# Windowed attention with sinks, then a gated MLP: another layout for keys and queries, turned in quarters, and another order of the stages

## The chip, the cores and the metric

The kernel runs on one core of a Trainium2 chip. The metric is the device time of one execution in microseconds, as a median of several executions. The core has TensorE (PE, matrix products; its weight loads are listed as PEld), VectorE (DVE), ScalarE (ACT), GpSimd (POOL) and SyncE (SP, which here issues DMAs). Each engine works through its own instructions in order and waits for others through semaphores.

## The reference

There are 4 batches with 8 heads, 768 positions and head dimension 64, all in float32. Each query sees the first 4 positions (the sinks) and its own 128 latest positions. The heads are put side by side to rows of 512 and go through a gated MLP with 1536 hidden columns.

```python
scores = scale * np.matmul(q, k.transpose(0, 1, 3, 2))
pos = np.arange(S)
is_sink = pos[None, :] < int(n_sink)              # n_sink = 4
rel = pos[:, None] - pos[None, :]
in_window = (rel >= 0) & (rel < int(window))      # window = 128
scores = np.where(is_sink | in_window, scores, -1000000000.0)
scores = scores - np.max(scores, axis=-1, keepdims=True)
a = np.exp(scores)
a = a / (np.sum(a, axis=-1, keepdims=True) + 1e-09)
attn = np.matmul(a, v)
x = attn.transpose(0, 2, 1, 3).reshape(B * S, H * D)
out = (np.maximum(x @ w_gate, 0.0) * (x @ w_val)) @ w_out
```

## The kernel before

**Units and stages.** A unit is a pair of heads of one batch; there are 16, four per batch, and unit i has batch i // 4. "Stage i.x" below is stage x of unit i. Every unit passes through these stages.

*Load and cast.* `load_kq` (L88) and `load_v` (L93) issue DMAs on SP: keys and queries as 96 partitions with 8 rows of each head (two runs of 2 KB per partition), V as seven overlapping tiles of 128 rows, 256 bytes a row, in three DMAs. `cast_kq` (L108) and `cast_v` (L102) turn them into bfloat16 on POOL. `cast_v` also copies the four sink rows of V into tiles 1, 3 and 5 (L106), on ScalarE for units 0 to 3 and on POOL later. There are three buffers for `kf` and `qf`, two for `kn` and `qn`, four for the others.

*T, the turn (L167).* TensorE turns keys and queries, so that the 64 dimensions of both heads lie on 128 partitions: 8 transposes for the keys and 8 for the queries, each of 96 partitions by 128 columns (L172). ScalarE copies the keys out of PSUM into `kE` (L178 to L181), where each block of 124 keys has the four sink columns ahead of it (L182 copies those). VectorE copies the queries into `qT` (L177).

*S, the scores (L185), in three groups g.* TensorE multiplies `kE` and `qT` per head, with 64 partitions of the array each and the two heads in two PSUM banks (L195). ScalarE takes the exponential (L199), VectorE multiplies with a mask (L201). For units 0 to 3 no such product is made; a bias is put into PSUM by a matmul first (L191).

*V, the output, in two halves of 384 columns (L205).* TensorE multiplies the weights `ee` with V and with ones (L212), one head in each column half of the array, first all products with V and then all with ones. VectorE turns the sums, takes the reciprocal, turns it back and multiplies (L218 to L222) into `xT`, the rows for the MLP. V 0 needs S 0 and S 1, and V 1 needs S 1 and S 2.

**PSUM.** Two pairs of banks, `PP`, serve T, S and V in turn; each stage takes the next pair by `pair()` or `two()`. S and V take one, while T takes two, one for the keys and one for the queries, and uses half of each. So a stage waits until the stage that used its pair has been read out. In the head T and V take single banks from `G` instead. `G` serves the MLP afterwards.

**MLP.** `chunk(b, g, m)` (L227) makes 128 hidden columns for 384 rows of batch b: four matmuls for the gate (L234), Relu on ScalarE (L237), four for the value (L239) and the product into `hT` on VectorE (L241). Its fourth matmul needs `xT` of the fourth unit. `ffn2` (L248) is one matmul of the last layer (L254); after twelve of them ScalarE copies the result (L258) and SP stores it (L259).

**Order.** The program order is written out by hand. First comes the head: T, S 0, S 1 and V 0 of units 0 to 3, S 2 of units 0 and 1, and the weight loads between them. Then 96 slots follow. Each slot holds one chunk, then the stages that `plan` gives it, then up to three `ffn2` matmuls (there are none before slot 24). Slots 0 to 5 hold what is left of units 0 to 3, V 3.1 in slot 5. The list `later` holds the stages of units 4 to 15, and its first 24 entries are spread over slots 6 to 23, the others go one to a slot:

```python
later += [("T", i, 0)] + [("S", i, g) for g in range(3)] + [("V", i, 0), ("V", i, 1)]
...
plan[6 + x * 18 // 24 if x < 24 else x].append(st)
```

So slot 6 holds T 4 and S 4.0, slot 7 S 4.1, slot 8 S 4.2, slot 9 both V of unit 4, slot 10 T 5, slot 11 S 5.0, slot 12 S 5.1 and S 5.2, slots 13 and 14 V 5.0 and V 5.1. Slots 15 to 23 repeat this for units 6 and 7, and slot 24 has T 8. Four slots ahead of a T, `front(i)` puts the casts of that unit and the loads of the next one into the order of POOL and SP; for units 5 and 6 the load waits behind a small write on POOL (`gate`), so that it starts only after the casts of the unit before.

Of the kernel before, what the change touches and what calls it, by code (L numbers as in the profile page):

```python
# [9 lines left out]
F32 = mybir.dt.float32  # L10
BF16 = mybir.dt.bfloat16
Alu = mybir.AluOpType
# [7 lines left out]
def kernel(  # L20
# [12 lines left out]
    nc = tc.nc  # L33
    B, H, S, D = q.shape
    assert (B, H, S, D) == (4, 8, 768, 64)
    NP = H // 2
# [3 lines left out]
    FM = d_ff // 128  # L40
    NR, PR = 8, 96

# [6 lines left out]
    NQ, NV, NE, NT = 3, 4, 4, 4  # L49
    kf = [const.tile([128, 2, 512], F32, name=f"kf{i}") for i in range(NQ)]  # L50
    qf = [const.tile([128, 2, 512], F32, name=f"qf{i}") for i in range(NQ)]
    vf = [const.tile([128, 7, 2, 64], F32, name=f"vf{i}") for i in range(NV)]
    vn = [const.tile([128, 7, 2, 64], BF16, name=f"vn{i}") for i in range(NV)]
    qT = [const.tile([128, S], BF16, name=f"qT{i}") for i in range(NT)]
    kE = [const.tile([128, 884], BF16, name=f"kE{i}") for i in range(NT)]
    ee = [const.tile([128, 3, 2, 512], BF16, name=f"ee{i}") for i in range(NE)]
    qn = [const.tile([128, NR, 2, 64], BF16, name=f"qn{i}") for i in range(2)]
    kn = [const.tile([128, NR, 2, 64], BF16, name=f"kn{i}") for i in range(2)]
    wg = const.tile([128, KO, d_ff], BF16, name="wg")
# [13 lines left out]

    SEG = [(503, [(0, 0, 0, 255), (128, 128, 255, 503)]),
           (499, [(252, 252, 0, 251), (380, 376, 251, 499)]),
           (415, [(504, 500, 0, 251), (632, 624, 251, 395), (756, 748, 395, 415)])]

    VSEG = [[(0, 0, 0, 255, 0), (1, 0, 255, 503, 128), (2, 1, 0, 132, 252), (3, 1, 251, 259, 376)],
            [(2, 1, 132, 251, 0), (3, 1, 259, 499, 0), (4, 2, 0, 251, 116),
             (5, 2, 251, 395, 240), (6, 2, 395, 415, 364)]]  # L80

# [4 lines left out]
    U = [Unit(i) for i in range(B * NP)]  # L86

    def load_kq(u):  # L88
        for x, dst in ((k, kf[u.i % NQ]), (q, qf[u.i % NQ])):
            nc.sync.dma_start(out=dst[0:PR, :, :],  # L90
                              in_=x[u.b, 2 * u.p:2 * u.p + 2].rearrange("h (p n) d -> p h (n d)", n=NR))

    def load_v(u):  # L93
        dst = vf[u.i % NV]
        for h in range(2):
            src = v[u.b, 2 * u.p + h]
            nc.sync.dma_start(out=dst[:, 0:6, h, :],  # L97
                              in_=bass.AP(src.tensor, src.offset, [[D, 128], [124 * D, 6], [1, D]]))
        nc.sync.dma_start(out=dst[0:24, 6, :, :],
                          in_=v[u.b, 2 * u.p:2 * u.p + 2, 744:768, :].rearrange("h s d -> s h d"))  # L100

# [6 lines left out]
    def cast_kq(u):  # L108
        for src, dst in ((kf[u.i % NQ], kn[u.i % 2]), (qf[u.i % NQ], qn[u.i % 2])):
            nc.gpsimd.tensor_copy(dst[0:PR], src[0:PR].rearrange("p h (n d) -> p n h d", d=64))  # L110

    def gate(u):

        nc.gpsimd.memset(kf[u.i % NQ][0:1, 0, 0:2], 0.0)

# [9 lines left out]
    def setup():  # L125
        nc.vector.memset(warm[:], 0.0)
        nc.scalar.activation(warm[:], warm[:], Act.Exp, bias=0.0, scale=1.0)
        make_identity(nc, ident)
        t0, a = msk[:, 0, 0:255], msk[:, 1, 0:251]
        for x, w, d in ((t0, 255, 0), (a, 251, 4)):  # L130
            nc.gpsimd.memset(x, 1.0)
            nc.gpsimd.affine_select(out=x, in_=x, compare_op=Alu.is_ge, fill=0.0, base=d,
                                    pattern=[[1, w]], channel_multiplier=-1)
            nc.gpsimd.affine_select(out=x, in_=x, compare_op=Alu.is_ge, fill=0.0, base=127 - d,
                                    pattern=[[-1, w]], channel_multiplier=1)
        cp, ms = nc.vector.tensor_copy, nc.vector.memset
        for i in range(NT):
            ms(kE[i][:, 780:884], 0.0)
        ms(ones[:], 1.0)
        ms(msk[0:4, 0, 0:128], 1.0)  # L140
        ms(msk[0:4, 0, 128:255], 0.0)
        ms(msk[0:4, 1, 0:124], 0.0)
        cp(msk[:, 0, 255:503], msk[:, 1, 0:248])
        ms(msk[0:4, 0, 255:503], 1.0)
        cp(msk[:, 1, 251:499], msk[:, 0, 255:503])
        cp(msk[:, 2, 0:251], msk[:, 1, 0:251])
        cp(msk[:, 2, 251:395], msk[:, 0, 255:399])
        cp(msk[:, 2, 395:415], msk[:, 1, 0:20])
        for g in range(3):
            n = SEG[g][0]  # L150
            nc.vector.tensor_scalar(mb[:, g, 0:n], msk[:, g, 0:n], -1.0, BIG, op0=Alu.add, op1=Alu.mult)
# [4 lines left out]
    def pair():  # L156
        rot[0] += 1
        return PP[rot[0] % 2]

    def two():  # L160
        if head[0]:
            srot[0] += 2
            return G[srot[0] % 4][:], G[(srot[0] + 1) % 4][:]
        x = pair()
        return x[:, 0, :], x[:, 1, :]

    def T(u):  # L167
        t = u.i % NT
        tk, tq = two() if head[0] else (pair()[:, 0, :], pair()[:, 0, :])
        for x, ps in ((kn[u.i % 2], tk), (qn[u.i % 2], tq)):  # L170
            for n in range(NR):
                nc.tensor.transpose(ps.bitcast(BF16)[:, 96 * n:96 * n + 96],  # L172
                                    x[0:PR, n, :, :].rearrange("p h d -> p (h d)"), ident[0:PR, 0:PR])
        vk, vq = (ps.bitcast(BF16)[:, 0:768].rearrange("d (b p) -> d p b", p=PR) for ps in (tk, tq))
        e = kE[t]
        to = lambda ap: ap.rearrange("d (p b) -> d p b", b=NR)
        nc.vector.tensor_copy(to(qT[t][:]), vq)  # L177
        nc.scalar.copy(to(e[:, 0:128]), vk[:, 0:16])  # L178
        for i in range(2):
            nc.scalar.copy(to(e[:, 132 + 252 * i:380 + 252 * i]), vk[:, 16 + 31 * i:47 + 31 * i])  # L180
        nc.scalar.copy(to(e[:, 636:780]), vk[:, 78:96])  # L181
        nc.scalar.copy(e[:, 128:884].rearrange("d (i c) -> d i c", c=252)[:, :, 0:4],  # L182
                       e[:, 0:4].unsqueeze(1).to_broadcast([128, 3, 4]))
# [77 lines left out]
    with tc.manual_schedule():  # L261
# [4 lines left out]
        setup()  # L266
        gp_copy, act_copy = nc.gpsimd.tensor_copy, nc.scalar.copy
        cast_kq(U[0])
# [8 lines left out]
        Sg(U[0], 1, bias=True)  # L277
        cast_v(U[0], act_copy)
        T(U[2])
# [4 lines left out]
        V(U[0], 0)  # L284
        cast_v(U[1], act_copy)
        T(U[3])
# [3 lines left out]
        V(U[1], 0)  # L290
        cast_v(U[2], act_copy)
        gate(U[4])
# [4 lines left out]
        V(U[2], 0)  # L297
        cast_v(U[3], act_copy)
        load_w(4, 8)
# [36 lines left out]
        for s, x in enumerate(first):  # L336
            plan[s].append(x)
        later = []
        for i in range(NP, len(U)):
            later += [("T", i, 0)] + [("S", i, g) for g in range(3)] + [("V", i, 0), ("V", i, 1)]  # L340
        for x, st in enumerate(later):
# [62 lines left out]
```

## Time and profile before

| | us |
|---|---|
| median of 11 executions | 284.74 (282.04 to 287.48) |
| the profiled execution, own time | 285.43 |
| its span, first to last instruction | 283.6 |
| TensorE busy | 257.9 (91%) |
| VectorE busy | 159.0 (56%) |
| ScalarE busy | 124.2 (44%) |
| GpSimd busy | 65.6 (23%) |
| first chunk (slot 0) starts at | 29.20 |
| slot 6 starts at | 42.21 |
| slot 24 starts at | 93.50 |

The span is cut into 40 slices of 7.1 us in the page's second part, and a digit there is a tenth of the slice. In timeline lines the columns are start, duration of the group, engine, line, operation, output <- inputs, shape and count; in brackets stands how long the engine was idle before, and what ended this. Matmuls overlap in the array, so durations of a group reach beyond the start of the next. In lines of waits the columns are who waited for whom, us in total, times, and the longest.

### The profile page before, as it was taken

The page shows a single profiled execution, that of the slowest core. Times are in us where ns is not written, and L with a number is a line of the kernel's source. Part 1 is how long each engine was busy: PE and PEld are TensorE (multiplying, and loading weights), DVE is VectorE, ACT ScalarE, POOL GpSimd, SP SyncE. Part 2 cuts the span into 40 slices and gives each one's busy share as a digit, 9 for nine tenths or more (in the row PEclk, how much of TensorE's full clock was granted, in tenths as well). Part 3 has the DMA queues.
Part 4 walks back from the last instruction along what each step waited for, and adds up shares of the span by engine and source line. Part 5 has one row for each costly group of instructions (what it writes and reads, how often), then busy time and mean ns, then how long its engine had stood idle before and what let it go on. Part 6 is the DMA issues. An engine that isn't in the chain of part 4 may idle for free.

```text
span 283.6 us, 5367 instructions
## 1 busy us (share of the span) xinstructions
PE 257.9 (91%) x2114; PEld 144.5 (51%) x2136; DVE 159.0 (56%) x298; ACT 124.2 (44%) x254; POOL 65.6 (23%) x86
## 2 busy tenths in 40 slices
PE   1896895979779899999999999999999999999994
PEld 0443563545345556464555555555645555555441
DVE  6257574578497858485757766575848233232100
ACT  3468333445435362636363654446262322323221
POOL 6684242520663400044004230220000000000000
PEclk9999997899799999999999999999999999999999
DMA  7999949599995000447117810900010010010122
GB/s 205 261 225 236 202 94 225 91 217 232 223 216 107 0 16 23 137 103 175 39 43 166 195 49 0 207 37 18 23 39 31 6 39 38 37 39 37 74 82 103
DMA packets 41992, 30.42 MB, mean 107 GB/s; under 512 B 27120, under 2 KB 32752, under 8 KB 41968
## 3 DMA queue, kind: packets, MB, share of 16 engines
q1 hardware_dynamic: 36160, 25.37, 37.0%
q0 software_dynamic: 5808, 4.72, 10.6%
q8 instruction: 16, 0.26, 0.4%
q14 instruction: 8, 0.07, 0.1%
HBM read 28.51 MB, written 6.29 MB: 123 GB/s over the span
## 4 chain that ended last, share of the span: by engine, by line
PE 67%; DMA 18%; DVE 4%; SPq 2%; ACT 2%; POOL 2%; issue 2%; POOLq 0%; ACTq 0%
PE g L254 19%; PE g L234 17%; PE g L239 17%; DMA vf<-in_v_dram 16%; PE pp L212 4%; PE pp L254 4%; PE pp L195 3%; DMA qf<-in_q_dram 2%; PE pp L172 2%; ACT ee L199 2%; SPq L90 1%; POOL vn L104 1%; SPq L97 1%; DVE R L220 1%; DVE t L218 1%
## 5 line engine op out<-in xcount | busy, mean ns | idle before, releaser
L237 ACT ACTIVATE gs<-g 128x384 f32<-128x384 f32 x96 | 47.1, 491 | 92.3 <-PE g L234 91.5
L241 DVE TENSOR_TENSOR hT<-gs,g 128x384 bf16<-128x384 f32 x96 | 53.0, 552 | 60.2 <-PE g L239 59.2
L234 PE MATMUL g<-xT,wg 128*128 128x384 bf16 x384 | 79.9, 331 | 3.7 <-DVE xT L222 3.7
L239 PE MATMUL g<-xT,wv 128*128 128x384 bf16 x384 | 79.6, 331 | 0.0
L254 PE MATMUL g<-wo,hT 128*128 128x512 bf16 x218 | 61.2, 381 | 1.6 <-issue 0.6
L199 ACT ACTIVATE ee<-pp 128x1006 bf16<-128x1006 f32 (+2 forms) x48 | 45.4, 957 | 24.2 <-PE pp L195 24.2
L234 PEld LDWEIGHTS <-wg 128*128 128x128 bf16 x384 | 35.9, 98 | 34.3 <-issue 4.3
L239 PEld LDWEIGHTS <-wv 128*128 128x128 bf16 x384 | 38.0, 99 | 27.7 <-issue 3.4
L201 DVE TENSOR_TENSOR ee<-ee,msk 128x1006 bf16<-128x1006 bf16 (+2 forms) x36 | 26.4, 733 | 24.6 <-ACT ee L199 24.5
L254 PEld LDWEIGHTS <-hT 128*128 128x128 bf16 x288 | 24.5, 98 | 24.8 <-issue 3.3
L110 POOL CAST kn<-kf 96x1024 bf16<-96x1024 f32 x16 | 16.6, 1035 | 78.9 <-DMA kf<-in_k_dram 56.9
L104 POOL CAST vn<-vf 128x896 bf16<-128x896 f32 x16 | 15.2, 951 | 29.7 <-DMA vf<-in_v_dram 29.2
L195 PE MATMUL pp<-qT,kE 64*128 64x251 bf16 (+4 forms) x224 | 18.9, 263 | 2.3 <-DVE qT L177 2.3
L110 POOL CAST qn<-qf 96x1024 bf16<-96x1024 f32 x16 | 16.8, 1050 | 11.2 <-DMA qf<-in_q_dram 8.9
L220 DVE STREAM_TRANSPOSE R<-r 128x384 f32<-128x384 f32 x32 | 18.5, 578 | 1.1
L258 ACT COPY ot<-g 128x512 f32<-128x512 f32 x20 | 11.7, 583 | 15.8 <-PE g L254 15.8
L218 DVE STREAM_TRANSPOSE t<-pp 128x384 f32<-128x384 f32 x28 | 16.2, 580 | 3.0 <-PE pp L212 2.1
L212 PEld LDWEIGHTS <-vn 128*64 128x64 bf16 x288 | 12.3, 109 | 10.5 <-issue 9.0
L195 PEld LDWEIGHTS <-kE 64*128 64x128 bf16 x224 | 7.4, 95 | 19.0 <-issue 14.4
L222 DVE TENSOR_TENSOR xT<-pp,R 128x384 bf16<-128x384 f32 x28 | 15.6, 558 | 1.0
L212 PE MATMUL pp<-ee,vn 128*64 128x251 bf16 (+8 forms) x256 | 14.5, 238 | 0.2 <-DVE ee L201 0.2
L212 PE MATMUL pp<-ee,ones 128*64 128x251 bf16 (+8 forms) x256 | 13.7, 233 | 0.0
(56 smaller groups left out, 149.9 us busy)
## 6 DMA issues: line engine op xcount, KB each, us to landing
kf<-in_k_dram SPq DMA_DIRECT2D x16, 384.0 KB
qf<-in_q_dram SPq DMA_DIRECT2D x16, 384.0 KB
vf<-in_v_dram SPq DMA_DIRECT2D x32, 192.0 KB
out_dram<-ot SPq DMA_DIRECT2D x24, 256.0 KB
wo<-in_moe_w_out_dram POOLq DMA_DIRECT2D x3, 512.0 KB, 11.1
wg<-in_moe_w_gate_dram POOLq DMA_DIRECT2D x2, 512.0 KB, 8.7
wv<-in_moe_w_val_dram POOLq DMA_DIRECT2D x2, 512.0 KB, 11.5
wg<-in_moe_w_gate_dram POOLq DMA_DIRECT2D x2, 256.0 KB, 6.1
```

The lines of the kernel that those rows point to most:

```text
L110: nc.gpsimd.tensor_copy(dst[0:PR], src[0:PR].rearrange("p h (n d) -> p n h d", d=64))
L195: nc.tensor.matmul(out=ps[:, h, c0:c1], lhsT=kE[t][64 * h:64 * h + 64, x0:x0 + 128], rhs=qT[t][64 * h:64 * h + 64, q0:q0 + c1 - c0], start ...
L199: nc.scalar.activation(x, ps[:, :, 0:n], Act.Exp, bias=0.0, scale=scale)
L201: nc.vector.tensor_tensor(x, x, msk[:, g, 0:n].unsqueeze(1).to_broadcast([128, 2, n]), op=Alu.mult)
L212: nc.tensor.matmul(out=(pv, pd)[which][64 * h:64 * h + 64, o0:o0 + c1 - c0], lhsT=w, rhs=ee[u.i % NE][:, g, h, c0:c1], start=i == 0, stop= ...
L218: nc.vector.transpose(out=t1[:], in_=pd[:, 0:CUT])
L220: nc.vector.transpose(out=R[:].rearrange("p (c e) -> p c e", e=32), in_=r[:].unsqueeze(2).to_broadcast([128, CUT // 32, 32]))
L234: nc.tensor.matmul(out=gp[:, 0:CUT], lhsT=wg[:, ko, m * 128:(m + 1) * 128], rhs=x[:, ko, c], start=ko == 0, stop=ko == KO - 1)
L237: nc.scalar.activation(gs[:], gp[:, 0:CUT], Act.Relu, bias=0.0, scale=1.0)
L239: nc.tensor.matmul(out=vp[:, 0:CUT], lhsT=wv[:, ko, m * 128:(m + 1) * 128], rhs=x[:, ko, c], start=ko == 0, stop=ko == KO - 1)
L241: nc.vector.tensor_tensor(h[:, m, c], gs[:], vp[:, 0:CUT], op=Alu.mult)
L254: nc.tensor.matmul(out=op, lhsT=hT[b % 2][:, m, t * 128:(t + 1) * 128], rhs=wo[:, m, :], start=m == 0, stop=m == FM - 1)
```

## The change

Keys and queries lie 12 rows to a partition: head 0 on partitions 0 to 63, head 1 on 64 to 127, one run of 3 KB each. T then turns quarters of 64 by 64: for each of the 12 rows one quarter per head, so 24 for the keys and 24 for the queries. The quarters of the two heads use different row halves and column halves of the array and write different partitions of one PSUM bank. Keys and queries of one T take the two banks of one PSUM pair.

The key blocks are cut so that sinks lie at columns 120, 376 and 632; the tables SEG and VSEG, the masks and the loads of V follow from that. V comes in six DMAs. After the head, the copy of the queries out of PSUM is on ScalarE instead of VectorE. In the head, the copies of V's sink rows are on VectorE instead of ScalarE.

The list `later` has a new order: T of a unit stands ahead of V 0 and S 2 of the unit before, and V 1 of a unit stands between S 0 and S 1 of the next. Slots 6 to 24 then hold: T 4 and S 4.0; S 4.1; T 5; V 4.0 and S 4.2; S 5.0; V 4.1; S 5.1 and T 6; V 5.0; S 5.2; S 6.0 and V 5.1; S 6.1; T 7; V 6.0 and S 6.2; S 7.0; V 6.1; S 7.1 and T 8; V 7.0; S 7.2; S 8.0. V 7.1 is in slot 25. `front` still comes four slots ahead of each T.

```diff
-    NR, PR = 8, 96
+    NR, PR = 12, 64
...
-            nc.sync.dma_start(out=dst[0:PR, :, :],
-                              in_=x[u.b, 2 * u.p:2 * u.p + 2].rearrange("h (p n) d -> p h (n d)", n=NR))
+            nc.sync.dma_start(out=dst[:], in_=x[u.b, 2 * u.p:2 * u.p + 2].rearrange("h (p n) d -> (h p) (n d)", n=NR))
...
-        for h in range(2):
-            src = v[u.b, 2 * u.p + h]
-            nc.sync.dma_start(out=dst[:, 0:6, h, :],
-                              in_=bass.AP(src.tensor, src.offset, [[D, 128], [124 * D, 6], [1, D]]))
+        ld(dst[:, 0, :, :], 0, [[D, 128], [S * D, 2], [1, D]])
+        for t0, row, cnt in ((1, 116, 3), (2, 244, 2)):
+            for h in range(2):
+                ld(dst[:, t0:t0 + 2 * cnt, h, :].rearrange("p (i e) d -> p i e d", e=2)[:, :, 0, :],
+                   row + h * S, [[D, 128], [252 * D, cnt], [1, D]])
...
-            nc.gpsimd.tensor_copy(dst[0:PR], src[0:PR].rearrange("p h (n d) -> p n h d", d=64))
+            nc.gpsimd.tensor_copy(dst[:], src[:])
...
-        tk, tq = two() if head[0] else (pair()[:, 0, :], pair()[:, 0, :])
+        tk, tq = two()
         for x, ps in ((kn[u.i % 2], tk), (qn[u.i % 2], tq)):
             for n in range(NR):
-                nc.tensor.transpose(ps.bitcast(BF16)[:, 96 * n:96 * n + 96],
-                                    x[0:PR, n, :, :].rearrange("p h d -> p (h d)"), ident[0:PR, 0:PR])
+                for h in range(2):
+                    r = slice(64 * h, 64 * h + 64)
+                    nc.tensor.transpose(ps.bitcast(BF16)[r, 64 * n:64 * n + 64], x[r, 64 * n:64 * n + 64], ident[r, r])
...
-        nc.vector.tensor_copy(to(qT[t][:]), vq)
-        nc.scalar.copy(to(e[:, 0:128]), vk[:, 0:16])
+        nc.scalar.copy(to(e[:, 0:120]), vk[:, 0:10])
         for i in range(2):
-            nc.scalar.copy(to(e[:, 132 + 252 * i:380 + 252 * i]), vk[:, 16 + 31 * i:47 + 31 * i])
-        nc.scalar.copy(to(e[:, 636:780]), vk[:, 78:96])
-        nc.scalar.copy(e[:, 128:884].rearrange("d (i c) -> d i c", c=252)[:, :, 0:4],
+            nc.scalar.copy(to(e[:, 124 + 256 * i:376 + 256 * i]), vk[:, 10 + 21 * i:31 + 21 * i])
+        nc.scalar.copy(to(e[:, 636:780]), vk[:, 52:64])
+        (nc.vector.tensor_copy if head[0] else nc.scalar.copy)(to(qT[t][:]), vq)
+        nc.scalar.copy(e[:, 120:888].rearrange("d (i c) -> d i c", c=256)[:, :, 0:4],
                        e[:, 0:4].unsqueeze(1).to_broadcast([128, 3, 4]))
...
-        gp_copy, act_copy = nc.gpsimd.tensor_copy, nc.scalar.copy
+        gp_copy, ve_copy = nc.gpsimd.tensor_copy, nc.vector.tensor_copy
...
-        cast_v(U[0], act_copy)
+        cast_v(U[0], ve_copy)
...
-        later = []
+        later = [("T", NP, 0)]
         for i in range(NP, len(U)):
-            later += [("T", i, 0)] + [("S", i, g) for g in range(3)] + [("V", i, 0), ("V", i, 1)]
+            later.append(("S", i, 0))
+            if i > NP:
+                later.append(("V", i - 1, 1))
+            later.append(("S", i, 1))
+            if i + 1 < len(U):
+                later.append(("T", i + 1, 0))
+            later += [("V", i, 0), ("S", i, 2)]
+        later.append(("V", len(U) - 1, 1))
```

## The prediction

> **What bounds the kernel now.** I read the page's forty slices first, to see where TensorE is not the bound.
>
> ```profile
> PE   1896895979779899999999999999999999999994
> PEclk9999997899799999999999999999999999999999
> DMA  7999949599995000447117810900010010010122
> PE 67%; DMA 18%; DVE 4%; SPq 2%; ACT 2%; POOL 2%; issue 2%; POOLq 0%; ACTq 0%
> ```
>
> From slice 13 on (about 92 us) TensorE is full; the holes and the lower clock lie before that. The table of stretches says the same in us.
>
> ```profile
> 42.20:93.50 51.30, 42.77 (x413) 24.93 (x409) 36.91 (x67) 23.56 (x50) 20.11 (x24) 0.90 0.96 183
> 93.50:219.50 126.00, 123.75 (x1055) 69.94 (x1068) 84.91 (x151) 61.52 (x125) 21.18 (x24) 1.00 0.28 72
> ```
>
> The columns are the stretch, its length, busy us of PE, PEld, DVE, ACT and POOL, clock, DMA share, GB/s. In the second, TensorE work is path, one to one. In the first it idles at clock 0.90. DMA share is 0.96 there and the chain charges DMA 18%, so I asked TensorE's own waits between 42.2 and 97.3 us.
>
> ```profile
> PE pp L172 <- DVE xT L222: 4.2, 4, 1.5
> PE pp L195 <- DVE qT L177: 2.3, 2, 1.1
> PE g L234 <- DVE xT L222: 1.9, 1, 1.9
> PE pp L172 <- POOL vn L104: 1.0, 1, 1.0
> PE pp L212 <- DVE ee L201: 0.2, 1, 0.2
> ```
>
> No matmul waits for a load. The fourth line is one by name only: T does not read vn, and DVE's xT, whose PSUM buffer it takes, ended 0.05 us earlier. So the bound is the order T, S, V: a T that waits for V's buffer, an S that waits for the turn just before it. Such a wait also costs clock:
>
> ```profile
> 44.72 0.32 PE L234 MATMUL g<-xT,wg 128*128 128x384 bf16 x1 [1.85 <-DVE xT L222]
> ...
> 48.27 0.60 PE L195 MATMUL pp<-qT,kE 64*128 64x255 bf16 x4 [1.14 <-DVE qT L177]
> 48.81 1.46 PE L234 MATMUL g<-xT,wg 128*128 128x384 bf16 x4
> ```
>
> 1.46 us for four matmuls that take 0.81 elsewhere. I write stage i.x for unit i and count from slot starts (first L234 of each chunk): slot 6 at 42.21, slot 8 at 52.02, slot 24 at 93.50.
>
> **The turns.** Before:
>
> ```profile
> 111.30 0.51 PE L172 MATMUL pp<-ident,kn 96*128 96x96 bf16 x8
> ...
> 111.64 0.51 PE L172 MATMUL pp<-ident,qn 96*128 96x96 bf16 x8
> ```
>
> Eight turns in 0.34 us, 42.5 ns each; sixteen are 0.68. After, 48 quarters of 64 columns. A chunk runs 4 x 384 columns in 0.65 us, 2.37 a ns, so a quarter is 27 ns and some 2 for issue: 29. Do the two quarters of a pair run side by side? No row has quarters; the nearest are V's column halves.
>
> ```profile
> 123.14 0.81 PE L239 MATMUL g<-xT,wv 128*128 128x384 bf16 x4
> 123.88 0.53 PE L212 MATMUL pp<-ee,vn 128*64 128x119 bf16 x10
> 124.26 0.51 PE L212 MATMUL pp<-ee,ones 128*64 128x119 bf16 x10
> 124.71 0.82 PE L254 MATMUL g<-wo,hT 128*128 128x512 bf16 x3
> ```
>
> Ten matmuls, 119+240+251+144+20 = 774 columns per half, take 0.38 us. One half alone needs 774/2.37 = 327 ns, both in turn 654. They run side by side. So I take 24 x 29 = 0.69 us. Half-array work also pays at its edges: L239's four end at 123.14 + 0.65 = 123.79 and L212 starts 0.09 later; 124.26 + 0.38 = 124.64 and L254 starts 0.07 later. S pays 0.22 (slot 2.38 - chunk with three L254 1.95 - 503/2.37 ns). The old turns use the whole width and pay nothing. So T becomes 0.69 + 0.20 = **0.89 us, +0.21**. Below, 0.69 without edges. Above: the densest long run (two V back to back, 55.20 to 56.65) issued 72 loads and matmuls at 20 ns each, and T now has 96, so 1.93 us. I stay at 0.89, as the halves are the nearest row.
>
> The Trainium skill speaks against this: "TensorEngine Tiling (Array Packing)", section Restrictions and Gotchas, says that different row tiles cannot use one PSUM bank at the same time. Both quarters of a pair are different row tiles and write one bank, at other partitions. S puts its two row halves into two banks, so no row here tests the rule. By it a T would be 48 x 29 + 200 ns = 1.59 us, and the sum would end 8.4 us later.
>
> **The head, +0.95 us.** Slot 0 waits for V 3.0's xT, which ends at 29.15. Now ScalarE is blocked by a sink copy:
>
> ```profile
> 20.12 0.51 ACT L106 CAST vn<-vf 4x384 bf16<-4x384 f32 x1 [2.13 <-POOL vn L104]
> ```
>
> On VectorE this block ends for ScalarE, but the four copies join V's chain (L218 start to L222 end, 17.23 to 19.36: some 2.06 us). The copy there is in no row for VectorE; between 0.25 (the 251-column msk copy takes 0.22) and 0.96 (the 768-column qT copy), I take 0.45, near ScalarE's 0.51. Copy 1 follows vn's cast (end 20.08) to 20.55; qT of unit 3 to 21.50 (now 20.23); V 1.0's chain to 23.56; copy 2 to 24.0. From a copy's end to the next chain is 0.77 (20.63 to 21.40), so 24.78 to 26.84; copy 3 to 27.3; 28.07 to 30.1. That is 0.95 late; 0.45 to 2.0 for the two prices. The q and k loads reach the casts at some 1.45 us intervals (the wait before each is DMA's), so the smaller cast (768 elements per partition against 1024, near 0.85 against 1.04 us) buys nothing here.
>
> **Slots 6 and 7, +0.3 us.** Both orders put T 4 and S 4.0 into slot 6. V 3.1's wait of 1.85 stays. qT moves to ScalarE: its k copies and sinks now run 1.08 us from first to last (111.84 to 112.92); with 768 columns at their pace (248 in 0.26 us), 0.82 more, 1.90. Started after the k half, they end 0.3 later than now. 9.81 us becomes 10.1.
>
> **Slots 8 to 23, -4.6 us.** Now 41.48. Work after: 16 chunks at 1.30 (20.8), T 5 to 8 (3.56), V four firsts at 0.81 and three seconds at 0.93 (6.03), S 4.2 to 7.2 at 0.43, 0.42, 0.39 (4.11): 34.5. These costs are steady slots less 1.95, edges included. The T waits and T-then-S waits of slots 10, 15 and 19 go, and slot 16's slow chunk (3.00 against 1.72). What is late next: each item now needs the PSUM pair of the item before last. S 5.0 comes chunk plus S 4.2 (1.7 us) after V 4.0, whose chain needs 2.06 and stands behind a hT that waits for a Relu behind T's 1.90 on ScalarE: 0.85. S 7.0 likewise 0.8; T 6 and T 8 behind V x.1: 0.4 and 0.35. Sum 2.4, so 36.9. Bounds: no waits (-2.4), or one as long as today's at each (+3).
> Loads: V takes six DMAs instead of three (some 0.6 us of SP each), k and q 128 rows of 3 KB instead of 192 of 2 KB; bytes are the same. SP waits 170 us for L258, so the issues hide. T 6 comes near 64.9 (slot 8 at 52.02 + 0.95 + 0.3, then five chunks, 3.87 of stages and 1.25 of waits) and its casts ended at 61.2; T 7 another five chunks and 3.87 later, near 75.2, against 74.1. If loads land over 1 us later, that cover is gone, us for us.
>
> **From slot 24, +1.0 us.** T 8 is done (-0.68) and slot 24's T wait goes (3.77 - 2.63 = -1.14); V 7.1 is left (+0.93); V 7.0's xT is 0.4 late for the chunk; seven T cost 0.21 more (+1.47). VectorE and ScalarE have room in the second stretch. Mask shapes, 8 more columns a unit: under 0.2 in all.
>
> **Sum.** 0.95 + 0.3 - 4.6 + 1.0 = -2.35. The profiled execution took 285.43 (span 283.6), so 283.1; it stood 0.7 above the median of 284.74. On the median 282.4; I say **282.5**.
>
> **Rivals.** (1) *Order wins more*, 10%: none of the new waits and no head cost: -2.35 - 2.8 (2.4 and slot 24's 0.4) - 0.95 on 284.74, 278.6. For it: without four qT copies of 0.96 DVE drops from 36.9 to 33.1 us in that stretch. Against: V's chain is 2 us in every row. (2) *Quarters in turn*, 22%: the two of a pair do not overlap in one bank; 0.70 more for each of 12 T, all before a full TensorE: 282.5 + 8.4 = 290.9, slower. It decides once a T costs above 1.1 us (2.35/12 over 0.89). (3) *Issue-bound quarters*, 6%: 96 instructions at 20 ns, 1.93 us: 12 x 1.04 more, 295. (4) *Loads late*, 7%: T 6 to T 8 wait as long as the order gained: 287. My forecast, 55%, holds 279.5 to 285.5.
> A measurement of this kernel tells about 1% from no change. Inside the forecast I count half past -1% and half within; (1) is faster, (2) and (3) slower, (4) half slower: faster 0.37, same 0.32, slower 0.31. Range 279 to 291.
>
> **What would show it.** In the profile after: a T from first to last quarter in 0.7 us (right) or 1.4 (rival 2); pairs with nearly one start; steady T slots of 2.84 instead of 2.63; no wait of T for xT above 0.5; clock full after 52 us; L234's first at about 30.15 and slot 24 at 90. A T waiting for kn, a second clock hole, or Relu late in T slots would make me wrong.

## The result and the profile after

The changed kernel takes 289.87 us as a median of 12 executions (287.99 to 291.74), the kernel before 285.74 us in the same comparison (47 executions, 280.77 to 291.04). The ratio is 1.021 with a 95% interval of 1.018 to 1.024: slower by 2.1%. The prediction was 282.5 us, range 279 to 291, and its sign was wrong. The profiled execution took 290.20 us with a span of 288.5, against 285.43 and 283.6.

Executions of this kernel differ by the clock that TensorE is granted (before took 281.7 us at a mean clock of 0.998 and 285 to 288 at 0.976 to 0.99), and the ratios here leave out slower executions of each side, so that a ratio and the quotient of the two medians (1.014 for this result) can differ, most of all in `e2_weights_later`, `e3_six_v` and `e4_order_alone`, whose ratios work out to 281.7 us for before where its median is 286.76.

The page of the changed kernel, the forty slices and the chain by engine:

```profile
PE   2793698698998999999999999999999999999994
PEclk9999589899999999999999999999999999999999
DMA  7999879599970006420346006010000010010122
PE 80%; DVE 6%; DMA 6%; ACT 3%; issue 2%; POOL 1%; SPq 1%; ACTq 0%
```

The holes after slice 9 are gone, and the clock is at nine tenths or more from slice 8 on. But slices 4 and 5 (29 to 43 us) stand at 5 and 8 tenths of the clock, where before had 9. DMA has fallen from 18% to 6% of the chain. The table of stretches, cut at slots 6 and 24 of this kernel, with the columns of the prediction:

```profile
49.03:96.45 47.42, 40.96 (x569) 24.26 (x565) 31.11 (x60) 27.28 (x59) 19.62 (x26) 0.96 0.72 167
96.45:222.36 125.91, 123.34 (x1271) 69.32 (x1285) 75.36 (x141) 65.12 (x126) 16.18 (x20) 1.00 0.24 72
```

Slots 6 to 23 take 47.42 us instead of 51.30, at clock 0.96 instead of 0.90: the stretch that the new order was to shorten did become shorter. But it starts 6.82 us later. By slots (profiled executions, us):

| part | before | after | measured | predicted |
|---|---|---|---|---|
| slot 0 starts at | 29.20 | 34.22 | +5.02 | +0.95 |
| slots 0 to 5 | 13.01 | 14.81 | +1.80 | 0 |
| slots 6 and 7 | 9.81 | 9.70 | -0.11 | +0.3 |
| slots 8 to 23 | 41.48 | 37.71 | -3.77 | -4.6 |
| slot 24 to the end | 190.1 | 192.05 | +1.95 | +1.0 |
| sum | | | +4.9 | -2.35 |

Of the 7.2 us between sum and forecast, 5.9 lie ahead of slot 6. The timelines of SP, POOL and TensorE there; first the kernel before:

```profile
17.12 0.99 SPq L97 DMA_DIRECT2D vf<-in_v_dram  x2
...
17.52 0.88 POOL L118 DMA_DIRECT2D wg<-in_moe_w_gate_dram  x1
...
18.21 0.82 SPq L99 DMA_DIRECT2D vf<-in_v_dram  x1
...
22.87 0.93 POOL L104 CAST vn<-vf 128x896 bf16<-128x896 f32 x1 [0.44 <-DVE R L220]
...
25.69 0.66 PE L212 MATMUL g<-ee,vn 128*64 128x255 bf16 x8
...
29.20 0.81 PE L234 MATMUL g<-xT,wg 128*128 128x384 bf16 x4 [1.80 <-DVE xT L222]
```

and the changed kernel:

```profile
15.71 0.88 POOL L123 DMA_DIRECT2D wg<-in_moe_w_gate_dram  x1
...
17.80 3.13 SPq L98 DMA_DIRECT2D vf<-in_v_dram  x5
...
21.03 0.35 SPq L104 DMA_DIRECT2D vf<-in_v_dram  x1
...
29.50 0.93 POOL L109 CAST vn<-vf 128x896 bf16<-128x896 f32 x1 [6.26 <-DMA vf<-in_v_dram]
30.48 1.00 PE L218 MATMUL g<-ee,vn 128*64 128x247 bf16 x8 [5.33 <-POOL vn L109]
...
34.22 1.44 PE L240 MATMUL g<-xT,wg 128*128 128x384 bf16 x4 [0.86 <-DVE xT L228]
```

SP is busy for 3.6 us with the V of unit 3, before for 1.9; for units 1 to 3 it is 10.2 us (11.18 to 21.38) against 8.2 (10.81 to 19.03). The cast of unit 3's V comes at 29.50 instead of 22.87 and has waited 6.26 us for the load. TensorE waits 5.33 us for this cast, ahead of V 3.0, and runs slot 0 on a slow clock: 1.44 us for four matmuls that took 0.81.

### The profile page after: what moved, and what is told of

Same layout as the page of the kernel before. It is cut to its first block, busy times and chain, and to the rows that moved or that the text cites. A ratio compares the mean times of both kernels' runs of the same rounds, so it can differ in the third digit from the quotient of the medians.

```text
span 288.5 us, 6460 instructions
## 1 busy us (share of the span) xinstructions
PE 260.9 (90%) x2625; PEld 145.8 (51%) x2648; DVE 146.5 (51%) x287; ACT 131.5 (46%) x262; POOL 59.8 (21%) x87
## 4 chain that ended last, share of the span: by engine, by line
PE 80%; DVE 6%; DMA 6%; ACT 3%; issue 2%; POOL 1%; SPq 1%; ACTq 0%
PE g L240 20%; PE g L245 20%; PE g L260 19%; PE pp L218 7%; PE pp L201 4%; DMA vf<-in_v_dram 4%; PE pp L179 4%; PE pp L260 4%; DMA qf<-in_q_dram 2%; DVE t L224 2%; DVE R L226 2%; DVE xT L228 1%; PE pp L197 1%; ACT qT L187 1%; PE g L218 1%
## 5 line engine op out<-in xcount | busy, mean ns | idle before, releaser
L260 PE MATMUL g<-wo,hT 128*128 128x512 bf16 x219 | 60.5, 381 | 2.3 <-issue 1.9
L205 ACT ACTIVATE ee<-pp 128x998 bf16<-128x998 f32 (+2 forms) x48 | 46.0, 965 | 33.1 <-PE pp L201 32.9
L207 DVE TENSOR_TENSOR ee<-ee,msk 128x998 bf16<-128x998 bf16 (+2 forms) x36 | 25.0, 694 | 22.3 <-ACT ee L205 22.3
L115 POOL CAST kn<-kf 128x768 bf16<-128x768 f32 x16 | 13.7, 856 | 76.4 <-DMA kf<-in_k_dram 44.1
L201 PE MATMUL pp<-qT,kE 64*128 64x255 bf16 (+4 forms) x224 | 19.0, 262 | 3.9 <-DVE xT L228 2.0
L115 POOL CAST qn<-qf 128x768 bf16<-128x768 f32 x16 | 13.7, 855 | 7.4 <-DMA qf<-in_q_dram 6.8
L218 PE MATMUL pp<-ee,vn 128*64 128x255 bf16 (+8 forms) x256 | 14.7, 242 | 0.0
L179 PEld LDWEIGHTS <-kn 64*64 64x64 bf16 x384 | 8.2, 117 | 12.0 <-POOL kn L115 7.2
```

The lines of the kernel that those rows point to most:

```text
L115: nc.gpsimd.tensor_copy(dst[:], src[:])
L201: nc.tensor.matmul(out=ps[:, h, c0:c1], lhsT=kE[t][64 * h:64 * h + 64, x0:x0 + 128], rhs=qT[t][64 * h:64 * h + 64, q0:q0 + c1 - c0], start ...
L205: nc.scalar.activation(x, ps[:, :, 0:n], Act.Exp, bias=0.0, scale=scale)
L207: nc.vector.tensor_tensor(x, x, msk[:, g, 0:n].unsqueeze(1).to_broadcast([128, 2, n]), op=Alu.mult)
L218: nc.tensor.matmul(out=(pv, pd)[which][64 * h:64 * h + 64, o0:o0 + c1 - c0], lhsT=w, rhs=ee[u.i % NE][:, g, h, c0:c1], start=i == 0, stop= ...
L260: nc.tensor.matmul(out=op, lhsT=hT[b % 2][:, m, t * 128:(t + 1) * 128], rhs=wo[:, m, :], start=m == 0, stop=m == FM - 1)
```

## The experiments

**Theory A:** the six DMAs make V late; the more of V is left when the weight loads begin, the more. **Theory B:** the loads of V are no worse, but the weight loads start earlier (POOL issues the first at 15.71 instead of 17.52, since its casts are shorter) and take V's share of the DMA engines. **Theory C:** the copies of sink rows on VectorE delay the chain of the V stages.

**1. V in three DMAs.** In the changed kernel:

```diff
-        ld(dst[:, 0, :, :], 0, [[D, 128], [S * D, 2], [1, D]])
-        for t0, row, cnt in ((1, 116, 3), (2, 244, 2)):
-            for h in range(2):
-                ld(dst[:, t0:t0 + 2 * cnt, h, :]...
+        for h in range(2):
+            nc.sync.dma_start(out=dst[:, 0:6, h, :],
+                              in_=bass.AP(src.tensor, src.offset, [[D, 128], [124 * D, 6], [1, D]]))
```

> The changed kernel, with V loaded by three DMAs per unit, at the rows and in the form of the kernel before. (V's tiles then hold rows that do not fit the new key blocks, so the values are not those of the attention; sizes and the amount of work are the same.) Theory A, six DMAs per unit issue too slowly, so that V of units 2 and 3 is not there when the weight loads begin: V of the first four units has landed by about 22 us as before, V 3.0 starts near 27, slot 0 near 30 instead of 34.2 and slot 6 near 43 instead of 49; time near 284. Theory B, the weight loads are issued 1.8 us earlier because the casts are shorter, and that alone starves V: V 3.0 stays near 30 and the time near 289. Theory C, the sink copies on VectorE are the delay: slot 0 stays near 34, time 289 to 290.

Measured: 285.55 us (10 executions), ratio 1.002 (0.991 to 1.013), with the same quarters, order, sinks and casts. Its timeline:

```profile
22.44 0.93 POOL L107 CAST vn<-vf 128x896 bf16<-128x896 f32 x1 [3.00 <-DMA vf<-in_v_dram]
...
28.46 1.44 PE L238 MATMUL g<-xT,wg 128*128 128x384 bf16 x4 [0.87 <-DVE xT L226]
```

The cast of unit 3's V and slot 0 are as early as before, though the first weight load is issued at 14.12, still earlier than in the changed kernel. So earlier weights alone (B) don't make the loss, and neither do the sink copies (C): both are in this kernel, and by the medians it is 4.3 us faster than the changed kernel (in another comparison). The first chunk is on the slow clock nevertheless; more on that below.

**2. V in six DMAs in the kernel before.** Nothing else is changed.

```diff
-        for h in range(2):
-            nc.sync.dma_start(out=dst[:, 0:6, h, :], ...[124 * D, 6]...)
+        ld(dst[:, 0, :, :], 0, [[D, 128], [S * D, 2], [1, D]])
+        for t0, row, cnt in ((1, 124, 3), (2, 248, 2)):
+            for h in range(2):
+                ld(dst[:, t0:t0 + 2 * cnt, h, :]...[248 * D, cnt]...)
```

> The kernel before, with V loaded by six DMAs per unit, cut as the change cuts them, at the old rows. Theory A: V of unit 3 lands late here too, slot 0 comes 3 to 5 us later than 29.2 and the time is 289 to 291. Theory B: the weights start where they did, the time stays within 1 us of the kernel before (285.7). Both together: 1 to 3 us later.

Measured: 294.30 us (4), ratio 1.044 (1.032 to 1.055), 7.5 us (2.6%) above the median of before in the same comparison, and more than theory A expected.

```profile
30.47 0.93 POOL L106 CAST vn<-vf 128x896 bf16<-128x896 f32 x1 [4.06 <-DMA vf<-in_v_dram]
...
35.28 1.44 PE L236 MATMUL g<-xT,wg 128*128 128x384 bf16 x4 [0.89 <-DVE xT L224]
```

The cut alone does to the old kernel what the change did: slot 0 at 35.28, cold (on the slow clock; warm means at full clock). Of the 10.0 us between the spans of the two profiled executions 6.1 lie ahead of slot 0 and 1.6 in slots 0 to 5. Theory A holds from both sides.

**3. The weight loads two V casts later.** In the changed kernel, `load_w(0, 2)` follows `cast_v(U[2])` and `load_w(2, 4)` follows `cast_v(U[3])`.

> The changed kernel, with the first two pairs of weight loads put behind the casts of V of units 2 and 3 in POOL's order. Theories A and B both need the weights as the competitor: without them V of unit 3 lands by 23 us, slot 0 is near 30, slot 6 near 43, and the time is near 284. If six DMAs are slow by themselves, without any competition, V of unit 3 lands after 26 us and the time stays above 287. Theory C: 289 to 290.

Measured: 285.20 us (4), ratio 1.011 (1.002 to 1.020).

```profile
21.67 0.88 POOL L123 DMA_DIRECT2D wg<-in_moe_w_gate_dram  x1
...
23.31 0.94 POOL L109 CAST vn<-vf 128x896 bf16<-128x896 f32 x1
...
28.87 1.44 PE L240 MATMUL g<-xT,wg 128*128 128x384 bf16 x4 [1.40 <-DVE xT L228]
```

The weights are issued at 21.67; by then nearly all of V is there, V 3 is cast at 23.31 and slot 0 starts at 28.87. Six DMAs alone, with no weights beside them, are thus no loss of 5 us. Slot 6 starts at 46.87, where 43 was expected: in slot 4 TensorE waits 1.90 us for a tile of weights that now comes late. The profiled execution took 289.69, over 3 us more than the other three, and I read nothing later from it.

**The rates.** The records of the DMA packets say how fast V came (KB landed per us):

| | alone | beside the weight loads |
|---|---|---|
| six DMAs | 130 (e2_weights_later, 14 to 22 us) | 60 (after, 18 to 26), 67 (e3_six_v, 22 to 30) |
| three DMAs | 172 (before, 14 to 20; 206 from 15 on), 192 (e1_three_v, 12 to 16) | 94 (e1_three_v, 16 to 20), 96 (e4_order_alone, 22 to 26) |

A unit's V is 396 KB, and its six DMAs take SP 2.9 us (unit 2) to 3.6 to issue, 110 to 136 KB per us. They land alone at 130, so this fits a bound by their issue. In e3_six_v the six DMAs of unit 1 were all issued by 16.1 us, and there V landed at 198 KB per us from 16 to 18, as fast as in three; that speaks for the issue, but no run was made to test it. Beside the weights each form keeps about half of its rate, on the average of several us; single us lie between 12 and 238. The changed kernel had 530 of V's 1584 KB (units 0 to 3) left when the weights began to move, at 18 us, and 530/63 = 8.4 us bring it to 26.4; e1_three_v had 406 KB left at 16 us, and 406/95 = 4.3 us bring it to 20.3. The difference of 6.1 us stands against 7.1 between the two casts (29.50 and 22.44). Why the form with smaller DMAs gets less beside the weights, by its issue or by its size, no run here separates.

**4. The order alone.** In the kernel before: the new list `later`, both banks of a T from one pair, and the copy of the queries on ScalarE after the head.

```diff
-        tk, tq = two() if head[0] else (pair()[:, 0, :], pair()[:, 0, :])
+        tk, tq = two()
...
-        nc.vector.tensor_copy(to(qT[t][:]), vq)
...
+        (nc.vector.tensor_copy if head[0] else nc.scalar.copy)(to(qT[t][:]), vq)
...
-            later += [("T", i, 0)] + [("S", i, g) for g in range(3)] + [("V", i, 0), ("V", i, 1)]
+            later.append(("S", i, 0))
...
```

> The kernel before, with the new order of stages after the head, one PSUM pair per turn, and the queries copied by ScalarE after the head; layout, turns, loads of V and sink copies stay. If the steps on the order hold as the trace of the changed kernel shows them: slot 0 at 29.2 and slot 6 at 42.2 as before, slots 8 to 23 in 36.3 us instead of 41.5 (37.7 less four turns that cost 0.3 less), from slot 24 to the end 190 as before; time near 280.5, 1.8% faster than before. If the order's gain hung on the new layout, within 1 us of the kernel before.

Measured: 285.14 us (4), ratio 1.012 (1.008 to 1.016); the median of before in that comparison is 286.76, so time tells no gain here, and the expected 280.5 was missed. In the profiled execution slot 6 to the end takes 235.45 us instead of 241.4 (240.1 in the other profiled execution of before, below), some 5 less, and slots 8 to 23 take 38.20, where 36.3 was expected. But slot 0 started at 32.68, though nothing ahead of it was changed:

```profile
27.14 0.93 POOL L104 CAST vn<-vf 128x896 bf16<-128x896 f32 x1 [2.40 <-DMA vf<-in_v_dram]
```

In that execution the weights were issued at 19.82 and began to move at 21.5, with 396 KB of V left. The head of one and the same program moves by 3 us between executions, and with slot 0 cold as well slot 6 started 5.0 us later than in before, as much as the order brings.

**5. The kernel before, unchanged, as a run of its own.**

> The kernel before, unchanged, for a second profile of it. If the head is the same in each execution: slot 0 at 29.2 and slot 6 at 42.2 as in its first profile. If the head depends on how V and the weight loads meet in time, as the order-alone run suggests (slot 0 at 32.7 with the same head): slot 0 between 29 and 33, and whatever it is, slots 8 to 23 take 41.5 and the part from slot 24 on 190. Ratio 1.00.

Measured: 284.60 us (10) against 286.88, ratio 0.991 (0.986 to 0.997). Two runs of one kernel thus differ by 0.9%, and what follows can't claim a smaller gain. In its profile slot 0 starts at 29.66, slots 8 to 23 take 40.00 us, not the 41.5 of the first profile, and the part from slot 24 on 190.1.

**6, 7, 8. Order, weights, sinks and T 4, one after the other.** On `e4_order_alone`, first each weight load one V cast later; then the sink copies on VectorE as well; then T 4 ahead of V 3.1 in slot 5 as well.

```diff
-        load_w(0, 2)
         V(U[0], 0)
         cast_v(U[1], act_copy)
+        load_w(0, 2)
         T(U[3])
-        load_w(2, 4)
...
         cast_v(U[2], act_copy)
+        load_w(2, 4)
...
-        gp_copy, act_copy = nc.gpsimd.tensor_copy, nc.scalar.copy
+        gp_copy, act_copy = nc.gpsimd.tensor_copy, nc.vector.tensor_copy
...
+            if x == 0:
+                plan[5].insert(0, st)
...
```

> The order-alone kernel, with the first two pairs of weight loads one cast of V later in POOL's order each (behind the casts of V of units 1 and 2). If V left over at the start of the weight loads is what delays the head: V of unit 3 is cast before 25 us (27.1 in the order-alone run), slot 0 at 29 to 30.5, time 281 to 283. If the weights are then late for the first slots: a wait of a chunk's first matmul on a weight tile in slots 2 to 8, and no gain.

> As the run before, with the sink copies of the head on VectorE as the change has them. The prediction's step: slot 0 0.5 to 1 us later than in the run before. Against it the run with three V DMAs, whose slot 0 was at 28.5 with sinks on VectorE: slot 0 the same or up to 1 us earlier, because ScalarE no longer waits for V's cast.

> As the run before, with T 4 moved from slot 6 to slot 5, ahead of V 3.1. S 4.0 no longer waits for the turn (1.8 us in the changed kernel and in the order-alone run), the wait of slot 6's chunk for V 3.1 stays near 1.8 and a wait of V 3.1 for V 2.1's buffer of up to 1 us comes in slot 5: 1 to 2 us less than the run before, 279 to 282 in all, faster than both kernels.

Measured: 283.49 (ratio 0.988, 0.982 to 0.994), 284.01 (0.989, 0.982 to 0.995) and 282.95 us (0.988, 0.979 to 0.996), each of 4 executions and all in one comparison with the unchanged kernel of number 5 (284.60). They lie 0.6 to 1.7 us below it, and the lowest ratio is 0.4% under that of the unchanged kernel (0.991). T 4 in slot 5 has its local effect: slots 5 and 6 take 6.48 us instead of 8.50 in e6_order_weights, since the turn now lies ahead of V 3.1 and S 4.0 finds its keys. The profiled execution of e7_order_weights_sinks took 288.97, and I compare none of its slots; by the medians the sink copies cost 0.5 us there, within the spread.

The first and the last took longer than expected (281 to 283 and 279 to 282). In both a turn waits for its load, as the rival *Loads late* had it. Unit 7 in e6_order_weights:

```profile
76.16 0.51 PE L172 MATMUL pp<-ident,kn 96*128 96x96 bf16 x8 [1.57 <-POOL kn L110]
...
77.38 0.51 PE L172 MATMUL pp<-ident,qn 96*128 96x96 bf16 x8 [0.71 <-POOL qn L110]
```

These casts stand behind that of unit 6's V, which waits 8.82 us for its load. e8_turn_early loses 2.0 us in this way and e11_early_scalar (below) 3.6, while e4_order_alone, with the weights issued earlier, loses none. Slots 8 to 23 take 40.24, 39.91 and 42.03 us in these three, against 38.20.

**9. The changed kernel mended,** by the weights of number 6 and T 4 of number 8, with its six DMAs, quarters and sinks. **10. The changed kernel unchanged,** beside it.

> The changed kernel with two moves: the first two pairs of weight loads one cast of V later each (behind the casts of V of units 1 and 2), and T 4 in slot 5 ahead of V 3.1. Layout, quarters, six DMAs and sink copies are the change's. If V left over at the start of the weight loads is the delay: V of unit 3 is cast by 25 us instead of 29.5, slot 0 at 29.5 to 31, time 283 to 285, some 3 us (12 turns at 0.3) above the run with the whole turns, the same order and the same two moves. If six DMAs are slow whatever stands beside them: slot 0 stays past 32 and the time near 288.

> The changed kernel, unchanged, for a second profile of it. If its head is late for a cause that lies in the program: V of unit 3 is cast past 27 us and slot 0 past 32 again, turns at 0.98 us in the steady slots, time 288 to 291. If the first profile was an unlucky meeting of V and weights: slot 0 near 30 and a time near 285.

Measured: 283.81 us (10), ratio 0.999 (0.995 to 1.003), and 290.00 us (4), ratio 1.018 (1.009 to 1.027). The timeline of the mended kernel:

```profile
18.05 0.88 POOL L123 DMA_DIRECT2D wg<-in_moe_w_gate_dram  x1
...
25.26 0.93 POOL L109 CAST vn<-vf 128x896 bf16<-128x896 f32 x1 [1.97 <-DVE xT L228]
...
29.98 1.44 PE L240 MATMUL g<-xT,wg 128*128 128x384 bf16 x4 [0.87 <-DVE xT L228]
```

The loss repeats (in e10_after_again V 3 is cast at 28.08 and slot 0 starts at 32.80), and the two moves, of the weights' issue and of T 4, take 6.2 us back. In the traces, 4.2 us lie at the start of slot 0 (34.22 to 29.98; 2.8 against the profiled execution of e10_after_again, with 287.64 the shortest of its four), and 2.3 in slots 5 and 6 (6.55 instead of 8.89; 8.69 in e10_after_again). What is left of the change is worth nothing that can be measured against before.

**11, 12. The sinks back on ScalarE,** in e8_turn_early and in e9_mended. In all profiled executions with the copies on VectorE slot 0 was cold; before had it warm, though e3_six_v and e4_order_alone, with the copies on ScalarE, were cold too. In e1_three_v, with V there, V 3.0 stops for 1.45 us between its second and third product, since the third sink copy stands behind V 2.0's whole chain on VectorE. **Theory D** says that this stop lowers the clock.

```profile
23.42 0.30 PE L216 MATMUL g<-ee,vn 128*64 128x247 bf16 x2
25.17 0.55 PE L216 MATMUL g<-ee,vn 128*64 128x252 bf16 x6 [1.45 <-DVE vn L109]
```

```diff
-        gp_copy, act_copy = nc.gpsimd.tensor_copy, nc.vector.tensor_copy
+        gp_copy, act_copy = nc.gpsimd.tensor_copy, nc.scalar.copy
```

> Before's layout, loads and turns, with the new order, the weight loads one V cast later and T 4 in slot 5, and V's sink rows copied on ScalarE as before. It differs from e8_turn_early by the engine of these copies alone. Theory D: on VectorE the third copy stands behind the whole chain of V 2.0, so that the products of V 3.0 stop for 1.4 us (1.36 in e8_turn_early, 1.45 in e1_three_v, 1.57 in e7_order_weights_sinks), and the granted clock falls to 0.50 until slot 1: slot 0 takes 3.93 us there and 2.22 before. So here V 3.0 runs without that stop, the first four matmuls of slot 0 take 0.81 us instead of 1.44, slots 0 to 4 take 10.8 to 11.3 us instead of 12.5, and the median is 281.5, 1.0 to 1.7 below the 282.95 of e8_turn_early, ratio to before 0.98. Rival: the copies cost nothing, since ScalarE delays its exponentials by as much and slot 0 waits 1.8 us for xT either way; the clock falls at another place, and the median stays at 283.

> The changed kernel with the weight loads one V cast later and T 4 in slot 5, and V's sink rows copied on ScalarE. It differs from e9_mended by the engine of the copies alone. Theory D alone: as in e11_early_scalar, slot 0 warm, and a median 1.0 to 1.7 below the 283.81 of e9_mended, 282.4. Rival, the late V: with six DMAs V 3.0 waits for its load (2.45 us in e9_mended, of which 2.0 were the wait of the cast), and this wait alone lets the clock fall, so that slot 0 stays at 1.44 us and the median stays at 283.8.

Measured: 283.62 us (12), ratio 0.995 (0.992 to 0.998), and 283.78 us (11), ratio 0.994 (0.991 to 0.997): 0.7 above and level with the medians of the kernels they differ from (in other comparisons). The timeline of e11_early_scalar:

```profile
25.73 0.66 PE L212 MATMUL g<-ee,vn 128*64 128x255 bf16 x8
...
29.24 1.44 PE L234 MATMUL g<-xT,wg 128*128 128x384 bf16 x4 [1.80 <-DVE xT L222]
```

V 3.0 now runs its eight products without a stop, as theory D said, and slot 0 is cold all the same, after the same 1.80 us of waiting for `xT` that left it warm in the kernel before. Theory D falls. (The median of e12_mended_scalar is the one that the rival, the late V, expected.) Slot 0 takes 2.22 us where it is warm (before, e5_before_again, e6_order_weights) and 3.56 to 4.12 in the eleven other profiled executions, where it is cold.

What decides between them can be read from the traces. In each of them the granted clock changes only at points that lie whole multiples of 3.41 us apart, and where these points lie differs from execution to execution: before falls to half at 45.40, is back at 52.23, falls at 72.71 and is back at 76.12; in e11_early_scalar the four points are 28.87, 32.28, 76.66 and 80.07. From 22.5 us to slot 0 the matmuls of these two executions start within 0.05 us of each other. But 1.43 of the 1.80 us of waiting lie in the period of e11_early_scalar that ends at 28.87, where the clock falls, while in before a point at 28.34 cuts the wait into 0.94 and 0.86. The wait is not all: in e6_order_weights one period holds all 1.78 us of it, and the clock stays full. Two periods of e11_early_scalar (columns as in the tables of stretches):

```profile
25.46:28.87 3.41, 1.98 (x31) 1.27 (x31) 3.13 (x8) 2.14 (x4) 0.97 (x2) 1.00 1.21 223
28.87:32.28 3.41, 3.04 (x14) 1.38 (x15) 0.53 (x2) 0.49 (x1) 1.00 (x1) 0.50 1.12 235
```

and that of e6_order_weights:

```profile
28.14:31.55 3.41, 1.63 (x15) 0.92 (x14) 1.91 (x5) 1.35 (x2) 0.00 (x0) 1.00 1.15 266
```

TensorE is busy for longer in the period before the fall, but there it runs mostly V and S, which use half of the array per matmul, and in e6_order_weights chunks, which use all of it. As an estimate of the array's work I count each matmul's columns at 2.37 a ns, times the share of the array that it uses, as a part of 3.41 us: 0.36 in that period of e11_early_scalar, 0.41 in that of e6_order_weights, 0.47 and 0.67 in the two of before. In all 14 traces, from 9 us on, the clock fell after 24 of 28 periods at full clock with under 0.375 and after none of the 1016 with more. So the same sequence of matmuls can keep or lose its clock, by where the periods happen to lie. This is a count over the traces; no run was made to test it.

As e11_early_scalar and e12_mended_scalar are 0.5% below before, and the unchanged kernel was 0.9% below itself, none of the versions is shown to beat before.

## Why the prediction was wrong

**The head, +0.95: this step failed.** The prediction says of V's six DMAs "SP waits 170 us for L258, so the issues hide". That is a sum over the run, and all of the 170 us lie behind the head. In the head SP issues back to back, so each extra issue moves all later ones, and the last one ends 2.35 us later. The sentence weighed the loads of T 5 to T 8, for which the cover did hold in this execution (no wait for a load in slots 8 to 23), and never asked for V 3.0's load, which TensorE needs soon after its issue. The chain of the kernel before had the place in it:

```profile
11.99 6.32 DMA vf<-in_v_dram
```

These 6.32 us of V's load stand in the head (start and length, in us). The prediction read DMA's 18% of the chain, asked TensorE's waits only from 42.2 us on, and set the share aside. Behind it came what no row of before showed: the V that is left when the weights begin to move arrives at half its rate. With V in three DMAs and nothing else changed slot 0 starts at 28.46 instead of 34.22 and the median is 285.55 instead of 289.87 (e1_three_v). The rival *Loads late* put the wait at T 6 to T 8, and at 7%; its form was right and its place wrong.

"The smaller cast buys nothing here" was wrong in the other direction: with casts of 0.83 us instead of 1.04, and keys and queries that came at intervals of some 1.0 us where the prediction counted on 1.45, POOL issued the weights 1.8 us earlier, which with late V is a loss. With the weights issued at 18.05 instead of 15.71, e9_mended casts the same V 4.2 us earlier.

**The sink copies.** 0.41 us against 0.45 estimated (0.78 once, and 1.52 once in e1_three_v, while POOL issued weight loads). In e1_three_v they hold V 3.0 up as described, and slot 0 still starts at 28.46, no later than before. The 0.95 was not there.

**Slots 0 to 5, 0 predicted, +1.80.** All of it is the slow clock of slot 0 (4.01 us instead of 2.22): the clock falls at 27.78, in the wait of 5.33 us for V 3, and is back at 38.02. Late V is not needed for it, as e1_three_v and e11_early_scalar show.

**Slots 6 to 23: right in the waits, less sure in the gain.** The four waits that the prediction named are there, at the size it gave; TensorE's waits from 49 to 100 us in the changed kernel:

```profile
PE g L240 <- DVE xT L228: 2.1, 2, 1.7
PE pp L201 <- DVE xT L228: 2.0, 2, 1.0
PE pp L201 <- ACT kE L188: 1.9, 1, 1.9
PE pp L179 <- DVE xT L228: 0.8, 2, 0.4
```

The second line is S 5.0 and S 7.0, 1.0 us each (0.85 and 0.8 predicted), the last is T 6 and T 8 with 0.42 each (0.4 and 0.35). The third is S 4.0 behind ScalarE's copies, which the prediction had as T 4 and S 4.0 in one slot. Slots 8 to 23 became 3.77 us shorter, not 4.6: four turns at 0.09 more and 0.35 more for S 5.0 and S 7.0 are 0.7 of the 0.8. The second profiles give less: 40.00 us in e5_before_again, without the slow clock that before had from 72.71 to 76.12, and 38.51 in e10_after_again, so the gain lies between 1.5 and 3.8. Slots 6 and 7, too, go by the clock: 9.70 us here, at half clock from 55.09 to 58.50, and 8.18 in e10_after_again at full clock; before was at half in both of its profiles (9.81 and 10.00).

**The turns: right in kind, 0.09 short in size.** A steady slot with T and its groups:

```profile
120.97 0.81 PE L245 MATMUL g<-xT,wv 128*128 128x384 bf16 x4
121.72 0.57 PE L179 MATMUL pp<-ident,kn 64*64 64x64 bf16 x24
122.12 0.55 PE L179 MATMUL pp<-ident,qn 64*64 64x64 bf16 x24
```

The keys' 24 quarters start at 121.72 and the queries' at 122.12, so 24 quarters take 0.40 us. The steady slot is 2.93 us, so that T costs 0.98: 0.75 for 24 pairs at 31 to 32 ns and 0.23 at its edges, where the prediction had 29 ns and 0.20. The two quarters of a pair start 3 ns apart (121.717 and 121.720, the next pair at 121.770), and a pair takes 31 to 32 ns where one quarter's 64 columns need 27 at 2.37 a ns, so they run side by side. Rivals 2 and 3 (48 quarters in turn, 1.4 us; 96 instructions at 20 ns, 1.93 us) are both out.

The page "TensorEngine Tiling (Array Packing)" of the Trainium skill, section Restrictions and Gotchas, which spoke against the change, says that different row tiles cannot use one PSUM bank at the same time. These rows differ: two quarters in different row halves, writing other partitions of one bank, overlapped.

**From slot 24, +1.0 predicted, +1.95.** Seven turns cost 0.30 more each than before (2.93 against 2.63), 2.1 instead of 1.47: that is 0.6 of the 0.95. The kernels with the old turns and the new order take 189.9 us there (e6, e8, e11; 189.26 in e4_order_alone), so the quarters account for 192.05 - 189.9 = 2.1, and the order brought 0.2 where its terms in the prediction add up to 0.5: the other 0.3.

**In sum.** The order brought what it should in this pair of profiles, within 1 us, and less in others; the quarters cost about 1 us more than forecast over the eleven turns from slot 8 on; and the 4.1 us of head plus 1.8 us of clock, from a step that was costed at nothing, turned the sign.

## What to carry to other kernels

A queue's idle time over the whole run is no cover: ask in the stage itself how far ahead of its reader each DMA is issued, and count every issue in the head, where they stand back to back. A cheaper instruction on the queue that issues other loads moves these loads too, so look at what they will then meet; here the place of two pairs of weight loads, with one turn a slot earlier, was worth 6 us. Before trusting a gain of a few us, run the unchanged kernel once more as if it were a change: here that alone gave 0.9%.

## What the runs showed that was not expected

- 64x64 quarters on the diagonal run in pairs inside one PSUM bank, 31 to 32 ns a pair; and TensorE issued 96 weight loads and transposes in a row at 7.9 ns each (the turn of unit 3, from 16.99 us), where the densest long run that the prediction had found in before had 20 ns.
- V's rows of 256 bytes landed at 130 KB per us in six DMAs a unit and at 170 to 206 in three; beside the weight loads at 60 to 67 and at about 95.
- After the same wait of 1.80 us for `xT`, ahead of slot 0, the first chunk took 0.81 us for its four matmuls in the kernel before and 1.44 in e11_early_scalar: the granted clock changes at points 3.41 us apart, whose place differs between executions, and it fell only after periods with little array work.
- The start of slot 0 in kernels with the same head lay at 29.20, 29.66 and 32.68 us (before, e5_before_again, e4_order_alone): as large a difference as the order of the stages brought.
